# Retention and a cosine-gated MLP on one core: the second output weight is loaded earlier, block 3's retention is done in fewer visits, results get two buffers, loads run three blocks ahead

## The chip, the core and the metric

One core of one Trainium2 chip runs the whole program. The metric is the device time of one execution in microseconds (us), lower is better. Engines are named as in the profile: PE (TensorE's matmuls), PEld (its weight loads), DVE (VectorE), ACT (ScalarE), POOL (GpSimd) and SP (SyncE, which here only issues DMAs). Each engine works through its own instructions in the order in which the program lists them; engines wait for each other, and for DMAs, on semaphores.

## What is computed

Retention (attention with a decay in place of the softmax) for 8 batches, 8 heads, 576 positions and 64 features, and then a two-layer network on the 4608 tokens of 512 features. Types in and out are float32.

```python
def _attn_ref(q, k, v):
    scores = scale * np.matmul(q, k.transpose(0, 1, 3, 2))
    gamma = 1.0 - 2.0 ** (-5.0 - np.arange(H, dtype=np.float32))
    rel = pos[:, None] - pos[None, :]
    Dmat = np.where(rel >= 0, gamma[:, None, None] ** rel[None, :, :], 0.0)
    return np.matmul(scores * Dmat[None], v)

def _moe_ref(x, w_in, w_out):          # x: the retention's output, 4608 x 512
    h = x @ w_in                       # 512 -> 2048
    return (h * np.cos(h)) @ w_out     # 2048 -> 512
```

## The kernel before

**Tiling.** The tokens are cut in 18 blocks `j` of 256 (`BK`, two chunks of 128 each) for the retention, and in 9 stages `n` of 512 (`W`) for the network; stage n uses blocks 2n and 2n+1. Batches are 576 tokens long, so some chunks hold the end of one batch and the start of the next ("mixed", with masks and value tiles of their own: `mask_mix`, `mask_cmix`, `v_mix`, `v_odd`). Blocks 0 to 3 are laid out in pairs of positions (`c.pair`), later ones by chunk.

**A block's way.** `load` (L128) brings q, k and v into float32 tiles `fq`, `fk`, `fv` (pool `ld`, three buffers of each). `scaled` (L155) multiplies q and k by powers of the decay and rounds them to bf16 (`qks`); `prep` does that for all four parts on POOL. `transpose_dma` (L195) turns them by a DMA on SP, or `transpose_pe` (L203) on PE with an evacuation to `qkT` by ACT or DVE. `round_v` (L173) rounds v to `vb`. `scores` (L228) multiplies k by q into PSUM, and its two `masked` steps on DVE write `ret`. `sums_of` (L315) makes the state that is carried to the next chunk (`s32` on DVE, `sb` on ACT). `outputs` (L437) adds own and carried parts in PSUM and writes x (`xT`).

**The network.** `mm1` (L448) makes h for one part of a stage, ACT takes the sine (a shifted cosine), DVE multiplies (`gT`). For n = 0 the product with `w_out` is done directly (L878): 64 matmuls, with block 2's and block 3's retention steps placed in between by the list `todo`, which gives for each step the number of matmuls ahead of it. From n = 1 on, `mm2_seven` (L578) multiplies 2 x 2 quarters by seven products instead of eight, with sums of quarters of `gT` (`g_sum`, DVE, or POOL for sum 7 from n = 2 on) and of `w_out` (`w_sums`); results are gathered in tiles `ot` with tags a, b, c, d (pool `op`, one buffer of each tag) and stored by SP (`stored_rows`). The products run in the order 1, 2, 6, 4, 7, 5, 3; `at` says in front of which the retention steps of later blocks stand. `pend` holds DVE work and stores that `flush` issues later.

**What sets the order.** The schedule is written by hand (`manual_schedule`): program order is each engine's order. On SP the loads, the transposing DMAs and the stores stand in one queue. POOL issues the weights' DMAs (with the cast to bf16) between its own work. `step` (L645) does one block's preparation: `prep`, `transpose_dma`, `round_v` on POOL, and then `load_next`; `steps_to(j)` runs it up to block j - 1. At the start weights and loads are chained by `gate`s: block 2's load waits until the fourth part of `w_in` has landed (`w_dma[3]`), block 3's until the second part of `w_out` has (`w_dma[5]`). Four parts of `w_out` of four 128-row groups each are loaded (`load_w_out(0)`, `(4)`, `(8)`, `(12)`); the last two are issued after k and after q of block 2 are scaled (L779 to L782).

**Block 3** is turned on PE at the end of n = 0's products. Its scores are made in two visits, `scores_y` (L288), one for each parity of positions, inside the second and third part of n = 1's `mm1`, with two half-size DVE masks each; its sums stand in the fourth part, its outputs after that, and the fifth part is the first that needs its x.

```python
            if (n, i) == (1, 0):
                steps_to(5)
            ...
            steps_to({0: 7, 3: 8}.get(u, 0))                  # n = 1, after store u
            steps_to({0: 2 * n + 6, 2: 2 * n + 7}.get(u, 0))  # n > 1
```

The functions that the change touches, with the line numbers of the profile:

Of the kernel before, what the change touches and what calls it, by code (L numbers as in the profile page):

```python
# [17 lines left out]
def kernel(  # L18
# [10 lines left out]
    P = 128  # L29
# [34 lines left out]
    op = ctx.enter_context(tc.tile_pool(name="op", bufs=1))  # L64
# [9 lines left out]
    qpos_i = consts.tile([P, PERQ, 2, H], I32)  # L74
    qpos = consts.tile([P, PERQ, 2, H], F32)
    kpos_i = consts.tile([P, PERK, H], I32)
    kpos = consts.tile([P, PERK, H], F32)
    gq = consts.tile([P, PERQ, 2, H], F32)
    gkp = consts.tile([P, NP_B, 2, H], F32)
    gkc = consts.tile([P, PERK, H], F32)  # L80
    mask_p = consts.tile([P, 2, P], F32)
# [91 lines left out]
    def round_v(j, runs=(nc.gpsimd.tensor_copy,) * 2):  # L173
        f = tiles.pop(("fv", j))
        vb = nat.tile([P, 2, H, D], BF16, tag="vb", name="vb")
        for y in range(2):
            runs[y](vb[:, y], f[:, :, y, :] if j < NP_B else f[:, y])  # L177
        for c in chunks[j]:
            if c.mixed and c.pair:
                for y in range(2):  # L180
                    nc.gpsimd.tensor_copy(v_mix[HP // 2 : HP, y], f[HP // 2 : HP, :, y, :])
                    nc.gpsimd.tensor_copy(v_mix[HP:, y], f[HP:, :, y, :])
            elif c.mixed:
                nc.gpsimd.tensor_copy(v_odd[HP:], f[HP:, c.k])
        tiles["vb", j] = vb
# [101 lines left out]

    def scores_y(j, y, banks):  # L288

        cs = chunks[j]  # L290
        kT = tiles["qkT", j]
        if ("ret", j) not in tiles:
            tiles["ret", j] = retp.tile([P, 2, HG, 2, P], BF16, tag="ret", name="ret")
        ret = tiles["ret", j]
        mask = mask_mix if any(c.mixed for c in cs) else mask_p
        pss = [psum.tile([P, HG, P], F32, tag=t, name="sc") for t in banks]
        for hg in range(HG):
            for he in range(2):
                for c in cs:
                    nc.tensor.matmul(  # L300
                        pss[he][c.rows, hg, :],
                        lhsT=kT[he * D : he * D + D, 1, y, hg, c.rows],
                        rhs=q_cols(c, he, hg),
                        start=True,
                        stop=True,
                    )
        for he in range(2):
            nc.vector.tensor_tensor(
                out=ret[:, he, :, y, :],
                in0=pss[he],  # L310
                in1=mask[:, y].unsqueeze(1).to_broadcast([P, HG, P]),
                op=ALU.mult,
            )
# [461 lines left out]
    for r in range(2):  # L775
        late = slice(r * HP + HP // 2, r * HP + HP)
        nc.gpsimd.memset(mask_mix[: HP // 2, :, late], 0.0)
        nc.gpsimd.memset(mask_cmix[:HP, late], 0.0)
    for name in "kq":  # L779
        for y in range(2):  # L780
            scaled(nc.gpsimd, 2, name, y)
        w_dma += [load_w_out(8 + "kq".index(name) * 4)]  # L782
    round_v(2)
    load_next(names="kqv", gate=w_dma[5])
    load_next()
    prep(3)
    round_v(3)
# [20 lines left out]
    banks_of = {0: "mbmabmab", 1: "abmamabm"}  # L808
# [16 lines left out]

    def block3_sums():
        sums_of(3, "n")()()

    for n in range(NT):
        blocks = blocks_of.get(n) or [(e + k * E2, 0, W) for e in range(0, E2, 2) for k in range(2)]  # L830
        for i, (et, c0, cw) in enumerate(blocks):
            inside = {
                (0, 1): {1: block1_carried},
                (1, 1): {1: lambda: scores_y(3, 0, ("n", "st"))},
                (1, 2): {1: lambda: scores_y(3, 1, ("n", "st"))},
                (1, 3): {2: block3_sums},
# [6 lines left out]
            if (n, i) == (1, 3):  # L843
                outputs(3, "b")
                for e in range(0, E2, 2):
                    w_sums(7, e, e + 2)
            if (n, i) == (1, 4):
                steps_to(6)
            if (n, i) == (2, 2):
                steps_to(9)  # L850
            if n:
                sums_after(n, i)
        if n == 0:
# [5 lines left out]
                (12, lambda: transpose_pe(2, "k", "a", act)),  # L859
                (18, lambda: transpose_pe(2, "q", "b", act)),  # L860
                (24, block2_scores),
                (34, block2_sums),
                (46, lambda: outputs(2, "b")),
                (52, lambda: transpose_pe(3, "k", "a", act)),
                (59, lambda: transpose_pe(3, "q", "b", act)),
# [3 lines left out]
                for at, x, e in (  # L869
                    (4, 5, 0), (10, 5, 4), (50, 6, 0), (53, 6, 4), (57, 4, 0), (60, 4, 4)  # L870
# [3 lines left out]
            for done in range(4 * ET):  # L874
                while todo and todo[0][0] <= done:
                    todo.pop(0)[1]()
                e, t = divmod(done, 4)
# [7 lines left out]
            for t in range(4):  # L885
                ot = op.tile([P, 1, DM], F32, tag="abcd"[t], name="ot")
                (act, vec)[t % 2](ot[:, 0], pss[t])
                stored_rows(t * P, 0, DM, ot)
            load_next()
# [30 lines left out]
        def mid_unit(flush, pend):  # L920
            def then():
                flush()
                outputs(a, "m")

            intro(b, "ab", "st", pend, then)
# [16 lines left out]
        def stored(u):  # L942
            if n == 1:
                steps_to({0: 7, 3: 8}.get(u, 0))
            else:
                steps_to({0: 2 * n + 6, 2: 2 * n + 7}.get(u, 0))
# [32 lines left out]
```

## Time and profile before

The three timed runs took 313.01, 310.40 and 314.32 us: median 313.01. The profile is of one execution of its own.

| | |
|---|---|
| profiled execution, its time | 315.17 us |
| its span, first to last instruction | 313.5 us |
| mean granted TensorE clock | 0.976 of full |
| PE busy | 287.7 us (92%), 3256 instructions |
| DVE busy | 217.9 us (70%) |
| POOL busy | 151.7 us (48%) |
| ACT busy | 139.0 us (44%) |
| DMA moved | 49.78 MB, 159 GB/s over the span |
| q, k, v loads, stores, transposes (SP's queue) | 45.10 MB, 74.0% of the engines' time |
| weights (POOL's queue) | 4.19 MB, 8.2% |

Stages by PE, from the order of time (us from the span's start):

| stretch | what PE does |
|---|---|
| 0 to 17.6 | blocks 0 and 1 prepared, scored; weights arrive |
| 17.6 to 33.0 | first products of n = 0 |
| 33.0 to 56.5 | second products of n = 0, with blocks 2 and 3 between |
| 56.5 to 78.2 | first products of n = 1, with block 3's retention |
| 78.2 to 95.1 | second products of n = 1, with blocks 4 and 5 |
| 95.1 to 128.9 | n = 2 |
| 128.9 to 163.5 | n = 3 |
| 163.5 to 192.9 | n = 4; from here on each stage repeats this one |

How to read the lines further on. A row of the order of time has the start, the duration, the engine, the source line, the operation, what it writes and reads, the form, how many, and in brackets the idle time of the engine ahead of it with what ended it. A row of waits has who waited for whom, the total in us, how many times, and the longest. A row of windows has the stretch and its length, then busy us (and the instruction count) of PE, PEld, DVE, ACT and POOL, then the granted PE clock, the mean busy share of the 16 DMA engines (above 1 where packets overlap) and GB/s. When a wait was for several things, the row names the one that came last. A DMA row on SP (SPq) tells how long its issue took, not when the data landed.

### The profile page before, as it was taken

Reading aid. Unit: us, or ns where it says so; the run is one execution under the profiler, and the core shown is the slowest. Engines: PE = TensorE matmul, PEld = TensorE weight load, DVE = VectorE, ACT = ScalarE, POOL = GpSimd, SP = SyncE. Lnnn points to the kernel's source line nnn. Section 1 sums busy time; section 2 is a strip of 40 time slices with the busy share of each in tenths; the row PEclk is TensorE's granted clock in tenths of the full one; section 3 lists DMA queues with packets and bytes.
Section 4 is the critical chain, followed back from the end, with each engine's and each line's share of the span. In section 5 each row is a group of like instructions: output and inputs, shape, how many; then the busy total and the mean of one; then the engine's idle time right before and its main releaser. Section 6 shows DMA issues by size and latency. Waiting matters only on the chain.

```text
span 313.5 us, 7628 instructions
## 1 busy us (share of the span) xinstructions
PE 287.7 (92%) x3256; PEld 195.6 (62%) x3256; DVE 217.9 (70%) x267; ACT 139.0 (44%) x160; POOL 151.7 (48%) x180
## 2 busy tenths in 40 slices
PE   7689879879999988999599999999999999999991
PEld 3468534658875476547474587478648855874680
DVE  5656834565994997689365977797689669836931
ACT  4566413544344623365125633663364446326520
POOL 7830695942952974437902493269247113102300
PEclk9999998998999999999889999999999999999996
DMA  7999999699999999999998929995960630121014
GB/s 206 262 189 210 236 231 196 135 220 183 169 239 210 208 225 205 185 209 215 204 207 196 179 49 200 193 234 108 234 133 2 120 84 0 36 69 35 2 33 100
DMA packets 128930, 49.78 MB, mean 159 GB/s; under 512 B 89344, under 2 KB 128384, under 8 KB 128896
## 3 DMA queue, kind: packets, MB, share of 16 engines
q1 hardware_dynamic: 124672, 45.10, 74.0%
q0 software_dynamic: 4224, 4.19, 8.2%
q8 instruction: 25, 0.41, 0.6%
q14 instruction: 9, 0.07, 0.1%
HBM read 36.70 MB, written 9.44 MB: 147 GB/s over the span
## 4 chain that ended last, share of the span: by engine, by line
PE 66%; DMA 11%; DVE 10%; POOL 6%; issue 2%; ACT 2%; SPq 1%; DVEq 0%; POOLq 0%; ACTq 0%
PE h L458 29%; PE o L560 27%; DMA fk<-in_k_dram 5%; DVE gT L469 4%; POOL qks L166 4%; DMA w_in_sb<-in_moe_w_in_dram 3%; DMA w_out_sb<-in_moe_w_out_dram 3%; DVE gs L507 3%; PE o L878 3%; PE ov L388 2%; PE st L332 2%; ACT cosh L468 2%; DVE ret L278 2%; PE sc L268 1%; PE ov L420 1%
## 5 line engine op out<-in xcount | busy, mean ns | idle before, releaser
L458 PE MATMUL h<-xT,w_in_sb 128*128 128x512 bf16 (+1 forms) x704 | 128.8, 344 | 3.0 <-ACT xT L443 1.6
L469 DVE TENSOR_TENSOR gT<-h,cosh 128x1024 bf16<-128x1024 f32 x72 | 88.0, 1222 | 40.3 <-ACT cosh L468 40.1
L468 ACT ACTIVATE cosh<-h,half_pi 128x1024 f32<-128x1024 f32 x72 | 80.3, 1116 | 70.8 <-PE h L458 70.8
L458 PEld LDWEIGHTS <-w_in_sb 128*128 128x128 bf16 x704 | 69.2, 99 | 58.9 <-issue 1.5
L507 POOL TENSOR_TENSOR gs<-gT 128x512 bf16<-128x512 bf16 x28 | 35.8, 1282 | 96.4 <-DVE gT L469 96.4
L560 PEld LDWEIGHTS <-gs 128*128 128x128 bf16 x520 | 50.0, 99 | 11.3 <-issue 3.6
L166 POOL TENSOR_TENSOR qks<-fq,gq 128x512 bf16<-128x512 f32 x33 | 36.4, 1122 | 21.9 <-DMA fq<-in_q_dram 21.7
L560 PEld LDWEIGHTS <-gT 128*128 128x128 bf16 x384 | 37.1, 98 | 7.6 <-DVE gT L469 1.4
L590 ACT COPY ot<-o 128x512 f32<-128x512 f32 x32 | 18.7, 587 | 45.3 <-PE o L560 36.5
L560 PE MATMUL o<-w_out_sb,gs 128*128 128x256 bf16 (+1 forms) x264 | 32.2, 278 | 3.4 <-POOL qks L166 3.4
L586 DVE TENSOR_TENSOR ot<-ot,o 128x512 f32<-128x512 f32 x39 | 25.9, 681 | 12.4 <-ACT ot L590 7.9
L166 POOL TENSOR_TENSOR qks<-fk,gkc 128x512 bf16<-128x512 f32 x28 | 30.9, 1121 | 1.1 <-DMA fk<-in_k_dram 1.1
L560 PE MATMUL o<-w_out_sb,gT 128*128 128x256 bf16 x256 | 30.3, 273 | 1.1 <-DVE gT L469 1.1
L560 PE MATMUL o<-ws,gs 128*128 128x256 bf16 x256 | 30.8, 273 | 0.2 <-DVE gs L507 0.2
L278 DVE TENSOR_TENSOR ret<-sc,mask_c 128x1024 bf16<-128x1024 f32 x25 | 29.8, 1215 | 0.0
L177 POOL CAST vb<-fv 128x512 bf16<-128x512 f32 x33 | 21.5, 669 | 7.7 <-DMA fv<-in_v_dram 7.4
L443 ACT CAST xT<-ov 128x1024 bf16<-128x1024 f32 x16 | 16.2, 1012 | 15.6 <-PE ov L420 15.6
L362 DVE TENSOR_TENSOR s<-st,s 128x256 f32<-128x256 f32 x18 | 7.6, 423 | 17.2 <-PE st L332 16.8
L372 ACT CAST sb<-s 128x512 bf16<-128x512 f32 (+1 forms) x18 | 10.3, 575 | 18.7 <-DVE s L360 8.0
L878 PE MATMUL o<-w_out_sb,gT 128*128 128x512 bf16 x64 | 16.5, 401 | 2.2 <-DMA w_out_sb<-in_moe_w_out_dram 2.2
L507 DVE TENSOR_TENSOR gs<-gs,gT 128x1024 bf16<-128x1024 bf16 x16 | 15.8, 986 | 0.3
L560 PE MATMUL o<-ws,gT 128*128 128x256 bf16 x128 | 15.3, 272 | 0.0
(81 smaller groups left out, 199.3 us busy)
## 6 DMA issues: line engine op xcount, KB each, us to landing
out_dram<-ot SPq DMA_DIRECT2D x70, 128.0 KB, 2.6
fk<-in_k_dram SPq DMA_DIRECT2D x25, 256.0 KB, 5.5
fv<-in_v_dram SPq DMA_DIRECT2D x25, 256.0 KB, 5.9
fq<-in_q_dram SPq DMA_DIRECT2D x12, 512.0 KB, 4.9
w_in_sb<-in_moe_w_in_dram POOLq DMA_DIRECT2D x4, 512.0 KB, 8.3
w_out_sb<-in_moe_w_out_dram POOLq DMA_DIRECT2D x4, 512.0 KB, 11.2
fk<-in_k_dram SPq DMA_DIRECT2D x3, 512.0 KB, 7.1
fv<-in_v_dram SPq DMA_DIRECT2D x3, 512.0 KB, 7.3
```

Of the source, the lines that this page charges most:

```text
L166: return eng.tensor_tensor(out=dst.rearrange("p b a d -> p a b d"), in0=src.rearrange("p (a b) d -> p a b d", a=2), in1=by.rearrange("p (a ...
L177: runs[y](vb[:, y], f[:, :, y, :] if j < NP_B else f[:, y])
L278: nc.vector.tensor_tensor(out=ret[:, k].rearrange("p a b i -> p (a b) i"), in0=pss[k].rearrange("p a b i -> p (a b) i"), in1=mask.unsqueez ...
L443: evac(x, ps)
L458: nc.tensor.matmul(ps[:, j, :], lhsT=w_in_sb[:, dg, (et + j) * P : (et + j + 1) * P], rhs=xT[:, dg, c0 : c0 + w], start=(dg == 0), stop=(d ...
L468: nc.scalar.activation(cosh, ps, ACTF.Sin, bias=half_pi, scale=1.0)
L469: nc.vector.tensor_mul(gT[:, et : et + m, c0 : c0 + w], ps, cosh)
L507: eng.tensor_tensor(out=tiles["gs", n, x][:, e : e + step], in0=a[:, e : e + step], in1=b[:, e : e + step], op=op_,)
L560: nc.tensor.matmul(dst[i], lhsT=lhs[:, e, j * P : (j + 1) * P], rhs=rhs[:, e, c0:c1], start=(fresh and e == 0 and (i == 0 or len(parts) > 2)),
L586: return lambda: nc.vector.tensor_tensor(out=out_, in0=in0, in1=in1, op=ALU.add)
L590: nc.scalar.copy(t, tiles["all", x])
L878: nc.tensor.matmul(pss[t], lhsT=gT[:, e, t * P : (t + 1) * P], rhs=w_out_sb[:, e, :], start=(e == 0), stop=(e == ET - 1),)
```

## The change

- **Second weight ahead of the fourth block.** The third part of `w_out` is issued by POOL before block 2 is scaled, gated by the landing of the second part (`after`). The fourth part is issued between k and q of block 2. Block 3's load is gated by the third part (`w_dma[6]`) instead of the second. ("Fourth block" is block 3, counted from 1.)
- **Casts.** v of blocks 2 and 3 is rounded by ACT inside the list `todo`, not by POOL; `v_mix` is copied by DVE from the rounded tile in two copies, not by POOL from the float32 tile in four.
- **Retention of block 3 in fewer visits.** `scores_y` goes. All scores of block 3 are made at once after n = 0's products, with two full-size masks. Its sums move into the second part of n = 1's `mm1`, its outputs after the third part into bank `m`; the banks of that stage change.
- **n = 0's products.** The steps in `todo` move by some matmuls; the last quarter of the sum over rows of `w_out` is done result by result, and each of the four results is copied out when its last matmul is issued. The stores come after block 3's scores.
- **Two result buffers**: the pool `op` has two buffers of each tag. In exchange four small tiles used only at the start take the buffers of later `gs` tiles.
- **Loads three blocks ahead.** Blocks 5 and 6 are loaded from inside `todo`; before, block 5 was loaded after n = 0's stores. So each later `step` loads block j + 3 instead of j + 2.
- **Other places of preparations.** Block 8 is prepared after the last store of n = 1, not in the middle of n = 2's first products; block 7 after the third store; for n > 1 the second step of a stage comes after its last store instead of its third. `w_sums(7)` moves behind block 5's preparation.
- **Masks.** In n = 1 and 2 the second mask of the block scored in front of product 5 is no longer put off.

```diff
-    op = ctx.enter_context(tc.tile_pool(name="op", bufs=1))
+    op = ctx.enter_context(tc.tile_pool(name="op", bufs=2))
...
-    qpos_i = consts.tile([P, PERQ, 2, H], I32)
+    qpos_i = sump.tile([P, PERQ, 2, H], I32, tag="gs5", name="qpos_i")
...
             if c.mixed and c.pair:
-                for y in range(2):
-                    nc.gpsimd.tensor_copy(v_mix[HP // 2 : HP, y], f[HP // 2 : HP, :, y, :])
-                    nc.gpsimd.tensor_copy(v_mix[HP:, y], f[HP:, :, y, :])
+                nc.vector.tensor_copy(v_mix[HP // 2 : HP], vb[HP // 2 : HP])
+                nc.vector.tensor_copy(v_mix[HP:], vb[HP:])
...
+    w_dma.append(load_w_out(8))
+    after(w_dma[-1], w_dma[5])
     for name in "kq":
         for y in range(2):
             scaled(nc.gpsimd, 2, name, y)
-        w_dma += [load_w_out(8 + "kq".index(name) * 4)]
-    round_v(2)
-    load_next(names="kqv", gate=w_dma[5])
+        if name == "k":
+            w_dma.append(load_w_out(12))
+    load_next(names="kqv", gate=w_dma[6])
     load_next()
     prep(3)
-    round_v(3)
     prepared = 4
...
-    banks_of = {0: "mbmabmab", 1: "abmamabm"}
+    banks_of = {0: "mbmabmab", 1: "mababmab"}
...
+    def block3_scores():
+        for masked in scores(3, "ab"):
+            masked()
...
-                (1, 1): {1: lambda: scores_y(3, 0, ("n", "st"))},
-                (1, 2): {1: lambda: scores_y(3, 1, ("n", "st"))},
-                (1, 3): {2: block3_sums},
+                (1, 1): {1: block3_sums},
...
-            if (n, i) == (1, 3):
-                outputs(3, "b")
+            if (n, i) == (1, 2):
+                outputs(3, "m")
+            if (n, i) == (1, 4):
+                steps_to(6)
                 for e in range(0, E2, 2):
                     w_sums(7, e, e + 2)
-            if (n, i) == (1, 4):
-                steps_to(6)
-            if (n, i) == (2, 2):
-                steps_to(9)
...
-                (12, lambda: transpose_pe(2, "k", "a", act)),
-                (18, lambda: transpose_pe(2, "q", "b", act)),
-                (24, block2_scores),
-                (34, block2_sums),
+                (14, lambda: transpose_pe(2, "k", "a", act)),
+                (23, lambda: transpose_pe(2, "q", "b", act)),
+                (24, lambda: round_v(2, (act, act))),
+                (28, block2_scores),
+                (38, block2_sums),
                 (46, lambda: outputs(2, "b")),
+                (47, load_next),
+                (48, lambda: round_v(3, (act, act))),
                 (52, lambda: transpose_pe(3, "k", "a", act)),
-                (59, lambda: transpose_pe(3, "q", "b", act)),
+                (57, lambda: transpose_pe(3, "q", "b", act)),
+                (58, load_next),
...
-                    (4, 5, 0), (10, 5, 4), (50, 6, 0), (53, 6, 4), (57, 4, 0), (60, 4, 4)
+                    (4, 5, 0), (10, 5, 4), (44, 6, 0), (45, 4, 0), (50, 6, 4), (51, 4, 4)
...
-            for done in range(4 * ET):
+            part = 3 * ET // 4
+            order = [(t, e) for e in range(part) for t in range(4)]
+            order += [(t, e) for t in (2, 3, 0, 1) for e in range(part, ET)]
+            stores = []
+            for done, (t, e) in enumerate(order):
...
-            for t in range(4):
-                ot = op.tile([P, 1, DM], F32, tag="abcd"[t], name="ot")
-                (act, vec)[t % 2](ot[:, 0], pss[t])
-                stored_rows(t * P, 0, DM, ot)
-            load_next()
+                if e == ET - 1:
+                    ot = op.tile([P, 1, DM], F32, tag="abcd"[t], name="ot")
+                    (act, vec)[t % 2](ot[:, 0], pss[t])
+                    stores.append((t * P, ot))
+            block3_scores()
+            for r0, ot in stores:
+                stored_rows(r0, 0, DM, ot)
...
-            intro(b, "ab", "st", pend, then)
+            intro(b, "ab", "st", None, then)
...
-                steps_to({0: 7, 3: 8}.get(u, 0))
+                steps_to({0: 7, 2: 8, 3: 9}.get(u, 0))
             else:
-                steps_to({0: 2 * n + 6, 2: 2 * n + 7}.get(u, 0))
+                steps_to({0: 2 * n + 6, 3: 2 * n + 7}.get(u, 0))
```

## The prediction

> **What bounds the kernel now.** I read the chain of waits first, then who waits for whom, then the order of time between 33 and 164 us, and last the windows by stage. L(j) is the load of block j, T(j) its transposing DMA (L197), both on SP; times are us from the span's start.
>
> ```profile
> PE 66%; DMA 11%; DVE 10%; POOL 6%; issue 2%; ACT 2%; SPq 1%; DVEq 0%; POOLq 0%; ACTq 0%
> ```
>
> PE is the bound, but not everywhere. From 163.50 on one n of the main loop takes 29.44 (first-product starts 163.50, 192.94) and PE has no gap. Before that n=1 takes 38.6 (56.49 to 95.08), n=2 33.8, n=3 34.6. The change acts there, and the question is how much of each excess goes. The waits and the order of time name them:
>
> ```profile
> ACT ot L590 <- DMA out_dram<-ot: 7.0, 1, 7.0
> PE o L560 <- POOL qks L166: 3.4, 1, 3.4
> PE o L878 <- DMA w_out_sb<-in_moe_w_out_dram: 2.2, 1, 2.2
> PE h L458 <- ACT xT L443: 1.6, 1, 1.6
> ...
> 149.68 1.91 PE L560 MATMUL o<-ws,gT 128*128 128x256 bf16 x16
> 155.01 3.54 PE L560 MATMUL o<-w_out_sb,gs 128*128 128x256 bf16 x16 [3.42 <-POOL qks L166]
> ...
> 125.44 0.41 PE L388 MATMUL ov<-ret,vb 128*64 128x128 bf16 x8 [1.43 <-DVE ret L278]
> 111.47 1.70 PE L560 MATMUL o<-w_out_sb,gT 128*128 128x256 bf16 x14 [1.10 <-DVE gT L469]
> ```
>
> The first two rows are one event. In n=3 ACT's copy into `ot` (tag b) waits 7.0 until 154.38 for n=2's store of the same buffer, which SP issued behind T(10) and L(12) (issues from 140.69, the stores 149.96 to 153.17). PE can't add product 7 to the bank before that copy, so it stands 3.42; POOL is only who came last. The sixteen matmuls after it take 3.54, not 1.91: the clock falls after the gap.
>
> ```profile
> 70.00:74.00 4.00, 4.00 (x25) 2.99 (x24) 0.00 (x0) 0.79 (x1) 2.27 (x3) 0.62 1.08 160
> 156.00:160.00 4.00, 4.00 (x86) 2.80 (x83) 0.99 (x3) 0.92 (x2) 1.14 (x3) 0.70 1.00 201
> 124.00:126.00 2.00, 0.57 (x26) 0.47 (x27) 2.00 (x4) 0.00 (x0) 2.00 (x3) 1.00 1.33 218
> 126.00:130.00 4.00, 3.60 (x70) 2.47 (x59) 3.44 (x4) 1.32 (x2) 2.76 (x4) 1.00 1.00 181
> ```
>
> The clock (the column before the last two) is 0.62 after the 1.55 gap that ends at 69.58, 0.70 after the 3.42 one, and 1.00 after 1.43. So a PE gap of 1.55 or more costs 1.63 besides itself (3.54 - 1.91), one of 1.43 or less nothing. The Trainium skill, TensorE: Matmul & The Clock Gate, section on HAM oscillation, warns only of gaps above about 3.4 us; the 0.62 row speaks against it, and by the page the gaps I remove would be worth some 5 us less.
>
> The second limit is SP's one queue:
>
> ```profile
> 67.87 4.53 SPq L197 DMA_TRANSPOSE qkT<-qks  x1
> 72.46 0.62 POOL L177 CAST vb<-fv 128x512 bf16<-128x512 f32 x1 [0.32 <-DMA fv<-in_v_dram]
> 79.99 3.97 SPq L197 DMA_TRANSPOSE qkT<-qks  x1
> 84.47 1.02 POOL L177 CAST vb<-fv 128x512 bf16<-128x512 f32 x1 [0.18 <-DMA fv<-in_v_dram]
> 94.38 0.61 POOL L177 CAST vb<-fv 128x512 bf16<-128x512 f32 x1 [1.13 <-DMA fv<-in_v_dram]
> ...
> 55.50:58.50 3.00, 3.00 (x26) 2.21 (x24) 1.38 (x2) 1.99 (x3) 2.35 (x4) 1.00 0.13 27
> 64.00:72.40 8.40, 6.56 (x110) 4.77 (x108) 3.45 (x4) 3.64 (x4) 4.70 (x5) 0.84 1.16 203
> 84.40:94.40 10.00, 9.49 (x167) 7.94 (x166) 9.26 (x13) 4.55 (x7) 6.26 (x8) 1.00 1.19 227
> ```
>
> T(4)'s issue ends at 72.40, just when L(5)'s last v lands (the cast starts 72.46); T(5)'s at 83.96, as L(6) lands: a T waits for all that SP queued before it, then lands about 2 later. One L and one T take 10.4 (83.96 to 94.38), an L alone 7.6 (1.57 MB at 203 to 210 GB/s). Until 178 us the DMA engines are full, with one hole, 55.5 to 58.5 at 27 GB/s, in which SP waited for n=0's results to store.
>
> **Part by part.** (1) *Second weight.* L666 for rows 8 to 11 goes from POOL's place at 35.96 (landing 45.12) to just after rows 4 to 7 land (SP's gated L(3) shows that at 32.1). It then lands near 39 to 41 (first bytes 3.5 after its issue, then 0.52 MB at the 145 GB/s that its queue got between 40 and 46). POOL waits 13 us for that, beside a wait until 33.97 that it has anyway. PE's 2.17 at 45.16 goes, with the half clock behind it: 3.8. L(3) is now gated by this landing, so it starts near 40 instead of 32.14. That need not cost: L(2)'s v, and rows 12 to 15 issued at 36.0, fill the engines meanwhile, and the same 5.8 MB as before must pass from 29 to 55.5, so L(3) lands by about 49 to 51 and L(4) by 56 to 58 (before 57.9). By the queues' shares in 40 to 46 (POOL's 84.8% of the engines' time, SP's 34.2%) a weight goes ahead of a load, so block 2's v, which landed at 38.75, pays about 2.5. The Trainium skill, DMA: Bandwidth & Descriptors, section Queues, rings and completion order, has the engines take turns between the queues packet by packet; by that v would pay about half, and the weight would land a little later.
>
> (2) *Casts.* Four POOL casts (0.59 to 0.61) and four v_mix casts (0.61) leave POOL: 4.8 free, worth nothing by itself, for POOL then waits for L(3). Four ACT casts of 0.62 come, which wait for v; behind them in ACT stand the evacuations of block 3's transposes and the `ot` copies. With v(3) at 49 to 51, ACT has k and q out by 53 to 54.5. Two DVE copies of 1024 bf16 values: nearest rows 0.42 (512, from PSUM) and 0.69 (1024, two inputs); I take 0.4 each. They wait on DVE for ACT's cast of v(2) (near 42.5), and block 2's masks (2 x 1.2) stand behind them, done by 45.8; outputs(2) wants them at 46. Cover: 0.2; without it PE waits as long as v(2) is late, 1 to 2. The positions' tiles that now share `sump` buffers are read by 4 and overwritten at 65 at the earliest: nothing.
>
> (3) *n=0's products and block 3.* PE from 33.0: 64 matmuls at 0.214 to 0.23, 24 transposes and the rest of block 2 as before give 52.5; scores(3) waits for ACT until 53 to 54.5 and takes 0.64. First products of n=1 start at about 54 (before 56.49), and need 14.1 (128 at 0.11) + 0.75 sums + 1.4 outputs, for the two visits of scores (0.83 on PE, 1.0 of waits for DVE) are gone, and block 3's x is ready one whole product earlier, which removes the 1.55 and its 1.63. mm2 of n=1 could begin at 70.4, not 78.2: 7.8 on paper. DVE's four masks of 0.64 become two of 1.2: even.
>
> (4) *Loads three ahead.* This takes most of it back. Before T(4) SP now has L(5), L(6) and the eight stores; L(6) is new. From L(4) at 56 to 58: 7.6 + 7.6 + 2 to 4 for the stores puts T(4)'s issue at 74 to 77, landing 76 to 79 (before 74.2). The hole at 55.5 (3.0) is what this gains back. PE wants scores(4) at 74.3 (70.4 + 3.7 for two products + sums): a new wait of 2 to 4. T(5) comes 10.4 later, 86.4 to 89; PE would be there 9.3 after scores(4) (three products 5.75, sums and outputs 1.35, half clock 1.6, scores 0.6), so it waits again about 1. Scores(5) is at 86.4 to 88.5 against 89.25, and n=2 starts at 92.3 to 94.4 (5.8 later, as before) against 95.08: gain 0.7 to 2.8, taken 1.8. POOL's `w_sums(7)` (4 x 1.15) now stands behind block 5's preparation, ready about 71, wanted past 80: nothing, and it has 9 us of cover.
>
> (5) *n=2.* The second mask of blocks 5 and 7 is no longer put off behind the state sum that waits for PE: the 1.43 at 125.44 goes. Block 8's preparation leaves the middle of n=2, where POOL's own sums were late and DVE's took 1.08 and 1.62 beside them (0.69 at 173.01): the 1.10 at 111.47 goes, and 0.4 at 128.90 stays or goes. Gain 2.5. T(8) has to be there: T(5)'s issue 85.4 + 3 x 10.4 + 3 for stores = 119.6, landing 121.7; PE wants it at 93.3 + 28.4 = 121.7. No margin: 0 to 1 lost, 0.3 taken.
>
> (6) *Two result buffers.* n=3's copy meets a buffer last stored in n=1, and the step that stood before that store now follows it. 34.6 becomes 29.44, as in n=4, which has no such wait: gain 5.2. What is late next is nothing within that stage.
>
> Sum: 1.8 + 2.5 - 0.3 + 5.2 = 9.2. The profiled execution took 315.17 (span 313.5), 2.16 above the median 313.01, so 306.0 there and 303.8 on the median's footing; I say 304.
>
> **Rivals.** *A, the queue keeps the early gain.* If L's go at 182 GB/s (as in 72.4 to 84.4: 8.6 each), T(4)'s issue is at 58 + 17.2 + 4 = 79.2 and T(5) lands 11.4 + 2 later, 92.6: n=2 starts 3 late, and T(8) makes half of (5) void: 313.0 + 3 - 1.2 - 5.2 = 309.6, so 307 to 312. For: the 182 row. Against: 203 to 227 in the others.
>
> *B, slower: T(5) far behind.* L(3) behind the weight's landing, L(6) behind ACT's cast of v(3), T(4) behind both. It decides when scores(5) is past 89.25 + 7.4 + 6.3 = 103, 15 later than I have it. That takes L(3) starting 6 later (a weight held to 45 as before) and SP standing idle for one L more (7.6) while v(3) waits on ACT; then 319 to 324. Against: the engines were full in 40 to 46, so idle time must be new.
>
> *C, the early gain survives.* At 227 GB/s (6.9 an L) T(4)'s issue is at 56 + 13.8 + 2 = 71.8, T(5) lands 9.4 + 2 later, 83.2, and n=2 starts at 89, 6 early: 313.0 - 6 - 2.5 - 5.2 = 299.3, so 299 to 302.
>
> *D, the buffers move the wait*: ACT's copy then waits for something else in n=3; worth up to 5.2 back, 307 to 309. Against: n=4.
>
> **How the numbers follow.** Forecast 302 to 306.7: 0.50; C 0.11; A and D 0.23; B 0.16, 0.06 of it short of 2%. About 2% (6.3) is what a measurement of this kernel can tell from no change: faster (below 306.75) 0.61, within 0.29, slower 0.10. The range from C's 299.5 to near A's end, 311.5, leaves out some 0.2: most of B, the ends of A and C.
>
> **What would show it.** Right: no ACT wait on `out_dram<-ot`, n=3 at 29.5; T(4) landing after 74.2, PE waiting on scores(4) or (5) for a DMA; no gap at rows 8 to 11 of the weight. Wrong: first products of n=1 later than 56.5; scores(5) past 90; a new wait in n=2 on block 8; PE's clock below 1 in n=3.

## The result, and the profile after

The changed kernel took 310.2 us (median of 19 runs, 308.8 to 312.5), the kernel before 314.3 on the same chips: ratio 0.990, 95% interval 0.988 to 0.993. It is faster, by 1% where 2.9% was forecast. (Medians are of all runs; ratios and intervals leave out executions in a slower state, over 1.5% above the fastest of the same kernel.) The profiled execution took 312.25 (span 310.5, before 313.5).

Where the time went shows best in the starts of PE's stages, in the two profiled executions (us from the span's start; the forecast's lead is put together from its own terms):

| start of | before | after | lead forecast | lead measured |
|---|---|---|---|---|
| second products of n = 0 | 33.0 | 34.2 | 0 | -1.2 |
| first products of n = 1 | 56.5 | 55.9 | 2.5 | 0.6 |
| second products of n = 1 | 78.2 | 72.6 | 7.8 | 5.6 |
| n = 2 | 95.1 | 95.2 | 1.8 | -0.1 |
| n = 3 | 128.9 | 130.3 | 4.0 | -1.4 |
| n = 4 | 163.5 | 160.6 | 9.2 | 2.9 |
| end of the span | 313.5 | 310.5 | 9.2 | 2.9 |

The lead grows to 5.6, is lost altogether in 22 us, shrinks by another 1.3 in n = 2, and comes back by 4.3 in n = 3. From n = 4 on nothing changes. The chain's summary says what the end now waits for:

```profile
PE 68%; DMA 16%; POOL 5%; DVE 4%; issue 2%; ACT 2%; SPq 1%; DVEq 0%; POOLq 0%; ACTq 0%
```

DVE's share fell from 10% to 4%, and DMA's rose from 11% to 16%. Half of the 16% is the load of `w_out` (8%, before 3%), through which the chain now runs at the start; T's own share is 3%. What held PE is told by its waits (who for whom, total, times, longest):

```profile
PE sc L267 <- DMA qkT<-qks: 6.8, 3, 4.5
PE o L858 <- ACT ot L867: 2.2, 1, 2.2
...
PE h L430 <- DVE gT L441: 0.6, 1, 0.6
```

All three DMA waits are for a T. The rows of before that the prediction shows (the copy into `ot`, the weight, block 3's x) are gone from PE's waits, and one large row is new: a matmul of n = 0 waits 2.2 for a copy on ACT. The order of time, for PE, then ACT, then SP's queue:

```profile
52.16 1.24 PE L858 MATMUL o<-w_out_sb,gT 128*128 128x512 bf16 x5 [2.15 <-ACT ot L867]
...
81.00 1.07 PE L267 MATMUL sc<-qkT 64*64 64x128 bf16 x32 [4.54 <-DMA qkT<-qks]
...
89.80 0.64 PE L267 MATMUL sc<-qkT 64*64 64x128 bf16 x32 [0.21 <-DMA qkT<-qks]
...
125.95 1.07 PE L267 MATMUL sc<-qkT 64*64 64x128 bf16 x32 [2.03 <-DMA qkT<-qks]
...
50.49 1.14 ACT L177 CAST vb<-fv 128x512 bf16<-128x512 f32 x2 [1.27 <-DMA fv<-in_v_dram]
51.54 0.58 ACT L867 COPY ot<-o 128x512 f32<-128x512 f32 x1
...
65.24 4.53 SPq L149 DMA_DIRECT2D fv<-in_v_dram  x3
69.86 6.41 SPq L548 DMA_DIRECT2D out_dram<-ot  x8
76.37 2.30 SPq L196 DMA_TRANSPOSE qkT<-qks  x1
...
84.29 3.80 SPq L196 DMA_TRANSPOSE qkT<-qks  x1
...
120.15 3.67 SPq L196 DMA_TRANSPOSE qkT<-qks  x1
```

Read from the bottom. SP puts L(6) and then eight stores in front of T(4). L(6) lands at 72.48, the last store at 78.28, T(4)'s issue ends at 78.67 and it lands at 80.96; PE, ready at 76.46, waits 4.54 for it. T(5)'s issue ends at 88.09 and T(8)'s at 123.82, which lands at 125.91, 2.03 after PE wants it. The ACT rows explain the 2.15: the copy into `ot`, L867, stands in ACT's order behind the two casts of v(3), which wait for v(3) to land at 50.47. PE's next matmul writes the other half of the PSUM tile `two` that the copy reads from, and it does not start before the copy ends.

The windows (stretch, length, then busy us of PE, PEld, DVE, ACT and POOL; the granted clock is the column before the last two):

```profile
69.86:78.28 8.42, 6.60 (x67) 5.65 (x64) 8.28 (x10) 3.33 (x4) 6.54 (x7) 1.00 0.72 168
...
81.00:84.40 3.40, 3.40 (x44) 2.50 (x45) 2.71 (x3) 0.00 (x0) 0.80 (x1) 0.51 1.19 269
84.40:92.00 7.60, 7.39 (x125) 6.29 (x124) 4.34 (x6) 3.28 (x5) 5.33 (x6) 1.00 1.14 226
...
125.96:132.00 6.04, 5.82 (x51) 3.84 (x53) 3.04 (x3) 0.00 (x0) 0.00 (x0) 0.50 1.22 215
```

The stores' stretch moves 168 GB/s, less than the 203 and 227 of the loads' stretches that the prediction shows (its rival A names one of 182). After each wait the clock is at half, 3.41 us long the first time and 6.83 (125.29 to 132.12) the second, though that gap was the smaller.

### The profile page after: what moved, and what is told of

It is laid out like the page before. It is cut to its first block, busy times and chain, and to the rows that moved or that the text cites. A ratio compares the mean times of both kernels' runs of the same rounds, so it can differ in the third digit from the quotient of the medians.

```text
span 310.5 us, 7615 instructions
## 1 busy us (share of the span) xinstructions
PE 287.6 (93%) x3239; PEld 198.1 (64%) x3256; DVE 219.8 (71%) x267; ACT 140.7 (45%) x164; POOL 147.8 (48%) x172
## 3 DMA queue, kind: packets, MB, share of 16 engines
q1 hardware_dynamic: 124672, 45.10, 72.2%
## 4 chain that ended last, share of the span: by engine, by line
PE 68%; DMA 16%; POOL 5%; DVE 4%; issue 2%; ACT 2%; SPq 1%; DVEq 0%; POOLq 0%; ACTq 0%
PE h L430 32%; PE o L532 28%; DMA w_out_sb<-in_moe_w_out_dram 8%; POOL qks L166 4%; DMA qkT<-qks 3%; DMA fv<-in_v_dram 3%; DMA fk<-in_k_dram 2%; PE sc L267 2%; PE ov L360 2%; DVE gT L441 2%; PE st L304 1%; PE ov L392 1%; ACT cosh L440 1%; SPq L135 1%; PE o L858 1%
## 5 line engine op out<-in xcount | busy, mean ns | idle before, releaser
L430 PE MATMUL h<-xT,w_in_sb 128*128 128x512 bf16 (+1 forms) x690 | 127.5, 342 | 1.5 <-DVE gT L441 0.6
L441 DVE TENSOR_TENSOR gT<-h,cosh 128x1024 bf16<-128x1024 f32 x72 | 87.9, 1223 | 37.4 <-ACT cosh L440 37.2
L479 POOL TENSOR_TENSOR gs<-gT 128x512 bf16<-128x512 bf16 x28 | 35.7, 1277 | 105.5 <-DVE gT L441 103.6
L532 PEld LDWEIGHTS <-gs 128*128 128x128 bf16 x520 | 50.7, 100 | 8.0 <-issue 0.3
L166 POOL TENSOR_TENSOR qks<-fq,gq 128x512 bf16<-128x512 f32 x33 | 38.4, 1183 | 14.5 <-DMA fq<-in_q_dram 9.4
L532 PE MATMUL o<-ws,gs 128*128 128x256 bf16 x256 | 31.8, 279 | 0.0
L177 POOL CAST vb<-fv 128x512 bf16<-128x512 f32 x29 | 17.4, 624 | 1.6 <-DMA fv<-in_v_dram 1.6
L858 PE MATMUL o<-w_out_sb,gT 128*128 128x512 bf16 x61 | 14.6, 379 | 2.5 <-ACT ot L867 2.2
L267 PE MATMUL sc<-qkT 64*64 64x128 bf16 x448 | 9.6, 230 | 6.8 <-DMA qkT<-qks 6.8
L479 DVE TENSOR_TENSOR gs<-gT 128x512 bf16<-128x512 bf16 (+1 forms) x25 | 15.3, 612 | 0.4
```

The source lines that it names most:

```text
L166: return eng.tensor_tensor(out=dst.rearrange("p b a d -> p a b d"), in0=src.rearrange("p (a b) d -> p a b d", a=2), in1=by.rearrange("p (a ...
L430: nc.tensor.matmul(ps[:, j, :], lhsT=w_in_sb[:, dg, (et + j) * P : (et + j + 1) * P], rhs=xT[:, dg, c0 : c0 + w], start=(dg == 0), stop=(d ...
L441: nc.vector.tensor_mul(gT[:, et : et + m, c0 : c0 + w], ps, cosh)
L479: eng.tensor_tensor(out=tiles["gs", n, x][:, e : e + step], in0=a[:, e : e + step], in1=b[:, e : e + step], op=op_,)
L532: nc.tensor.matmul(dst[i], lhsT=lhs[:, e, j * P : (j + 1) * P], rhs=rhs[:, e, c0:c1], start=(fresh and e == 0 and (i == 0 or len(parts) > 2)),
L858: nc.tensor.matmul(pss[t], lhsT=gT[:, e, t * P : (t + 1) * P], rhs=w_out_sb[:, e, :], start=(e == 0), stop=(e == ET - 1),)
```

## The experiments

The theory: a T stands on SP behind everything queued before it, so the third load ahead delays T(4) and all later T by one L, and this gives back what the early edits gain; the two result buffers are most of what is left. Its rivals: the early edits gain nothing that lasts even without the third load; or what holds the kernel is the new wait on ACT, or the place of block 8, or the weight. All ratios are against the kernel before, run beside the kernel on the same chip (medians 314.0, 314.2 and 314.8 in the three groups of four runs). One table for all, with landings and starts from the profiles:

| kernel | T(4) | T(5) | T(8) | n=2 starts | n=4 starts | median us | ratio (95%) |
|---|---|---|---|---|---|---|---|
| before | 74.2 | 86.0 | 120.9 | 95.1 | 163.5 | 314.3 | 1 |
| after | 81.0 | 89.8 | 125.9 | 95.2 | 160.6 | 310.2 | 0.990 (0.988 to 0.993) |
| e1_two_ahead | 72.5 | 83.1 | 117.4 | 91.4 | 154.8 | 306.6 | 0.976 (0.972 to 0.981) |
| e2_before_two_buffers | 72.2 | 84.0 | 118.2 | 91.6 | 154.7 | 307.6 | 0.982 (0.975 to 0.988) |
| e3_after_one_buffer | 81.7 | 91.8 | 124.3 | 97.2 | 161.9 | 314.0 | 0.999 (0.995 to 1.003) |
| e4_transposes_on_act | 74.4 | 87.6 | 113.0 | 104.1 | 174.7 | 337.8 | 1.076 (1.070 to 1.081) |
| e5_two_ahead_v3_on_pool | 72.0 | 84.9 | 117.6 | 90.2 | 153.6 | 303.7 | 0.971 (0.964 to 0.978) |
| e6_block8_behind_sums | 71.7 | 82.9 | 118.3 | 88.3 | 150.6 | 302.2 | 0.965 (0.959 to 0.971) |
| e7_after_v3_on_pool | 79.7 | 88.5 | 124.7 | 94.6 | 158.1 | 309.6 | 0.989 (0.985 to 0.992) |
| e8_two_buffers_masks | 71.6 | 83.4 | 118.0 | 91.1 | 156.3 | 307.4 | 0.982 (0.976 to 0.988) |
| e9_weight_old_place | 70.3 | 81.0 | 117.3 | 88.1 | 149.6 | 302.3 | 0.963 (0.957 to 0.969) |
| e10_t5_ahead_of_load6 | 72.4 | 76.4 | 119.2 | 87.9 | 152.6 | 303.4 | 0.964 (0.959 to 0.969) |
| e11_masks_put_off | 72.0 | 84.6 | 116.8 | 91.4 | 153.3 | 305.3 | 0.966 (0.960 to 0.973) |
| e12_before_three_ahead | no record | 91.8 | no record | 99.5 | 161.5 | 312.1 | 0.992 (0.988 to 0.996) |

### The third load ahead: e1 and e12

The changed kernel without its second extra load:

```diff
                 (57, lambda: transpose_pe(3, "q", "b", act)),
-                (58, load_next),
```

> The changed kernel without the load of block 6 inside n = 0's products, so that every later step loads j + 2 as before the change. Theory Q (the gain is eaten because T(4) and T(8) stand behind one more load in SP's queue): T(4) lands near 70 to 72 instead of 80.96, PE has no DMA wait at scores(4) or scores(8), n = 2 starts near 90 instead of 95.4, and the time is 6 to 10 us below the changed kernel's 310.2 (300 to 304). Rival R (the DMA engines' throughput is the limit, so the order in the queue only moves the wait): T(4) is earlier, but T(5) and T(8) are not earlier than 88 and 124, PE waits there instead, and the time stays within 1.5 us of 310.2.

It is faster than the changed kernel: 0.976 against 0.990, intervals apart, some 4.4 us, less than the 6 to 10 expected. In its order of time:

```profile
52.47 1.24 PE L857 MATMUL o<-w_out_sb,gT 128*128 128x512 bf16 x5 [2.42 <-ACT ot L866]
...
108.73 2.36 PE L532 MATMUL o<-w_out_sb,gT 128*128 128x256 bf16 x20 [2.00 <-DVE gT L441]
...
67.90 2.18 SPq L196 DMA_TRANSPOSE qkT<-qks  x1
...
77.56 3.58 SPq L196 DMA_TRANSPOSE qkT<-qks  x1
```

T(4)'s issue ends at 70.08 and not 78.67, 8.6 earlier, one L; no scores wait for a DMA any more. n = 2 starts 3.8 earlier although the wait on ACT (2.42) is still there, with a half clock behind it this time. So T(4) is late in the changed kernel because of the extra load. What is next: the wait on ACT, and 2.00 on DVE in n = 2.

The other direction needs a kernel without the other edits: the kernel before with two buffers (e2, below), plus one load:

```diff
             load_next()
+            load_next()
             continue
```

> e2 (the kernel before with two result buffers, 307.6) with one more load, block 6, ahead of T(4) in SP's queue, nothing else of the change. Theory Q: T(4) lands near 80 instead of 72.2 and T(8) near 126 instead of 118.2; PE wants scores(4) at 78.5 and scores(8) at 122.4, so it waits about 1.5 to 4 at each, with half clocks: 4 to 8 us above e2, 311 to 315. Rival: the extra load costs only where PE comes early as in the changed kernel; here PE is late enough, and the time is within 1.5 of e2.

The ratio is 0.992 against e2's 0.982 (intervals just touching), 312.1 against 307.6 us in the medians. The order of time has the same picture as the changed kernel:

```profile
81.49 0.64 PE L268 MATMUL sc<-qkT 64*64 64x128 bf16 x32 [1.94 <-DMA qkT<-qks]
91.80 1.07 PE L268 MATMUL sc<-qkT 64*64 64x128 bf16 x32 [3.27 <-DMA qkT<-qks]
```

Both scores wait for their T, T(5) lands at 91.8 against 84.0 in e2, and n = 2 starts at 99.5 against 91.6. T(4)'s landing is not recorded in e12, but its issue ends at 79.45 against 70.56 in e2, and T(5) lands 7.8 later. So the delay by one load does not come from the other edits.

### The result buffers: e2 and e3

e2 is the kernel before with only this (and the four small start tiles in the buffers of `gs`, as in the change):

```diff
-    op = ctx.enter_context(tc.tile_pool(name="op", bufs=1))
+    op = ctx.enter_context(tc.tile_pool(name="op", bufs=2))
```

> The kernel before with two result buffers alone (and the four start tiles in the later tiles' buffers). By the prediction's term for the buffers n = 3 takes 29.4 instead of 34.6, and the time is 5.2 us below the kernel before, a ratio near 0.983. If the wait only moves (rival D), ACT or PE shows a new wait in n = 3 and the gain is under 2.5 us.

Ratio 0.982, some 5.8 us (1.2% to 2.5%); n = 3 takes 29.4 instead of 34.6. (Its profiled execution is 8.8 ahead at n = 4. The 3.6 beyond n = 3's share come earlier, where the half clocks that the kernel before had after its gaps at 45 and 70 did not come; they are not put down to the buffers.) These few words alone do as much as the whole change or more (0.982 against 0.990, intervals touching). The reverse, the changed kernel with one buffer of each tag:

```diff
-    op = ctx.enter_context(tc.tile_pool(name="op", bufs=2))
+    op = ctx.enter_context(tc.tile_pool(name="op", bufs=1))
```

> The changed kernel with one result buffer again. If the second buffer alone removed n = 3's stall, it comes back in n = 3 (about 5 us, 315). If the moved step (the store now stands ahead of the next block's transposing DMA and load) does it too, n = 3 stays at 29.5 to 30; but n = 1's last store now lands at 124.05 behind the load of block 10, after n = 2's copy into the same buffer at 117.2, so a wait appears in n = 2 instead, partly beside PE's wait for T(8): 2 to 5 us above 310.2.

Ratio 0.999, no difference from the kernel before; against 0.990 the second buffer is worth some 2.7 us in the changed kernel, half of what e2 has. The wait is back, but one stage earlier:

```profile
122.59 1.91 PE L532 MATMUL o<-w_out_sb,gs 128*128 128x256 bf16 x16 [3.36 <-POOL qks L166]
```

That is in n = 2 (before: the same gap at 155.01, in n = 3), and again ACT's copy behind it waits 3.94 on `out_dram<-ot`. Which stage meets the store depends on where the queue stands; with one buffer one stage does. Behind this wait PE comes to scores(8) later and does not wait for T(8) any more, so that n = 2 takes 35.3 in this profile and 35.1 in that of the changed kernel: one wait stands in the place of the other. Where the 2.7 lies is not shown.

### T on another queue: e4

The theory says that T waits only because SP's queue stands in front of it. The changed kernel with T issued by ACT:

```diff
         new_qkT(j)
-        nc.sync.dma_start(
+        nc.scalar.dma_start(
```

> The changed kernel with the transposing DMAs issued by ACT instead of SP, all else alike. Theory Q: T(4) no longer waits for loads 5 and 6 and the stores; it lands within 3 to 6 us of ACT's place for it (before 70), T(8) before 110, no PE wait for a DMA at scores(4) and scores(8), and the time is 300 to 305. Rival R: the engines are full, T lands late on any queue, and the time is within 1.5 us of 310.2. Against both: each issue stops ACT for as long as the transposing DMA waits for the engines; then ACT's sines come late and the time is above 310.

T(4) does land earlier, 74.4 against 81.0, but the kernel takes 1.076 of the time before. ACT's part of the order of time:

```profile
69.06 1.40 ACTq L196 DMA_TRANSPOSE qkT<-qks  x1
70.51 0.62 ACT L344 CAST sb<-s 128x512 bf16<-128x512 f32 x1 [8.35 <-POOL w_out_sb L459]
...
79.37 3.54 ACTq L196 DMA_TRANSPOSE qkT<-qks  x1
83.33 2.12 ACT L440 ACTIVATE cosh<-h,half_pi 128x1024 f32<-128x1024 f32 x2 [2.91 <-DVE gs L479]
...
86.36 4.18 ACTq L196 DMA_TRANSPOSE qkT<-qks  x1
...
97.91 5.07 ACTq L196 DMA_TRANSPOSE qkT<-qks  x1
...
103.30 4.06 ACTq L196 DMA_TRANSPOSE qkT<-qks  x1
107.46 1.11 ACT L440 ACTIVATE cosh<-h,half_pi 128x1024 f32<-128x1024 f32 x1 [3.42 <-issue]
```

Issuing a T holds ACT's own queue 1.4 to 5.1 us, and the sines and copies behind it are late. The issue is not all of it: around T(4) ACT computed nothing for 8.35, of which the issue is 1.40, and the row puts the wait down to POOL, which makes T's input; PE then waits 4.95, until 71.19, for the `sb` behind it. How the loss divides between the two was not tried. On SP the same issue holds up only other DMAs, so of the two queues SP is the better place for T; what stands ahead of it there is the question.

### The wait on ACT: e5 and e7

v(3) rounded on POOL behind `prep(3)`, as before the change, once in e1 and once in the changed kernel:

```diff
     prep(3)
+    round_v(3)
     prepared = 4
...
                 (47, load_next),
-                (48, lambda: round_v(3, (act, act))),
```

> Loads two blocks ahead as in e1, and v of block 3 rounded by POOL behind the preparation of block 3, not by ACT inside n = 0's products. In e1 PE stands 2.42 at 50.04 because the next matmul into the tile that holds two of the four results waits for ACT's copy of the first, and ACT waits for v(3). Theory: that gap goes, with the half clock that e1 shows behind it; n = 1 starts at 54 to 55.5 instead of 57.8, and the time is 2 to 4 us below e1's 306.6. Rival: T(4) (landing 72.5 in e1) then bounds scores(4), and less than 1 us is left.

> The changed kernel, loads three ahead, with v of block 3 rounded by POOL. It takes away the 2.15 wait at 50.01 alone. Theory Q: n = 1 starts 2 earlier, but scores(4) stays at T(4)'s landing, 80 to 81.5, so the wait there grows by as much and the time stays within 1.2 us of the changed kernel's 310.2. Rival: the unforeseen wait on ACT is what the forecast missed, and 2 to 4 us come back.

In both the gap at 50 is gone, and first products of n = 1 start at 54.3 and 54.6, where the prediction had them ("about 54"). With two loads ahead the median falls by 2.9 (306.6 to 303.7; the ratios' intervals, 0.971 and 0.976, overlap). With three ahead it falls by 0.6 (0.990 to 0.989), no difference that these runs can tell. There PE reaches scores(4) 1.3 earlier, T(4) also lands 1.3 earlier, and the wait is 4.59, with a half clock of 6.83 behind it; n = 2 starts 0.6 earlier. The wait on ACT is real, and with three ahead the wait for T(4) takes its place. With two ahead T(4) holds nothing up, but PE, now earlier, waits for T(5), which it had not done in e1:

```profile
84.91 0.64 PE L267 MATMUL sc<-qkT 64*64 64x128 bf16 x32 [3.00 <-DMA qkT<-qks]
```

### The place of block 8, and the masks: e6, e8, e11

e5 has a gap of 1.34 in n = 2 that comes from DVE's sums (L479), which take 1.39 and 1.63 beside POOL's work. e6 moves block 8's preparation behind them:

```diff
             if n:
                 sums_after(n, i)
+            if (n, i) == (2, 6):
+                steps_to(9)
...
-                steps_to({0: 7, 2: 8, 3: 9}.get(u, 0))
+                steps_to({0: 7, 2: 8}.get(u, 0))
```

> As e5, and block 8's preparation placed behind POOL's own sums in n = 2, not after the last store of n = 1. In e1 DVE's two sums beside POOL's take 1.63 and 1.62 instead of 0.68, and PE waits 2.00 for DVE at 106.7. Theory: POOL does its sums before DVE's, DVE's take about 0.7, the 2.00 goes and T(8), which stands behind load 9 anyway, lands no later than 119 (wanted at 120 or later): 1 to 2.5 us below e5. Rival: the two engines' sums overlap all the same, or T(8) comes late: within 0.7 of e5.

In n = 2 of e5, and then of e6, the order of time has these DVE rows:

```profile
101.60 1.39 DVE L479 TENSOR_TENSOR gs<-gs,gT 128x1024 bf16<-128x1024 bf16 x1
...
104.05 1.63 DVE L479 TENSOR_TENSOR gs<-gT,gs 128x1024 bf16<-128x1024 bf16 x1
```

```profile
99.56 0.68 DVE L479 TENSOR_TENSOR gs<-gs,gT 128x1024 bf16<-128x1024 bf16 x1
101.29 0.68 DVE L479 TENSOR_TENSOR gs<-gT,gs 128x1024 bf16<-128x1024 bf16 x1
```

The same instruction on the same tiles costs 0.68 or 1.63. In e5 POOL runs `scaled` from 97.95 to 102.4 and its own sums from 103.98 for 5.12, so it is at work when DVE's sums start. In e6 its sum there starts at 99.72, 0.16 after DVE's first, and it is POOL's that takes longer, 1.53 against 1.15 for its sum at 96.14; beside DVE's second POOL is idle, from 101.25 to 103.19. The Trainium skill, SBUF — State Buffer, section "SBUF: two separate sides", has DVE with two SBUF inputs and a GpSimd operation that reads SBUF lock a port pair against each other, and the one that starts later waits; the rows agree. The gap on the sums is gone, and the best version so far results: 302.2 us, 0.965. Against e5 (0.971) the intervals overlap; against the changed kernel and e1 they do not. What is left in PE's way is T again:

```profile
82.97 0.64 PE L267 MATMUL sc<-qkT 64*64 64x128 bf16 x32 [1.00 <-DMA qkT<-qks]
118.34 0.64 PE L267 MATMUL sc<-qkT 64*64 64x128 bf16 x32 [1.30 <-DMA qkT<-qks]
```

Then the masks that are no longer put off, alone on e2 (e8), and undone in e6 (e11):

```diff
-            intro(b, "ab", "st", pend, then)
+            intro(b, "ab", "st", None, then)
```

> The kernel before with two result buffers (e2, 307.6) and the second mask of the block scored ahead of product 5 no longer put off. The prediction's term: the 1.43 gap at the outputs of block 7 (120.38 in e2) goes and nothing else moves: 1.0 to 1.8 us below e2. Rival: DVE only shifts the wait, so that another stands behind it: within 0.5 of e2.

> e6 with the second mask of the block scored ahead of product 5 put off again, as in the kernel before. The prediction's term: a gap of 1.43 in front of block 7's outputs near 116, 1.0 to 1.8 above e6. Rival (as e8 on e2 suggested): PE then arrives later at scores(8), whose T(8) it waits for anyway (1.30), so the two overlap and the time is within 0.5 of e6.

In e8 the 1.43 shrinks to 0.32 and the time stays, 307.4 against 307.6: another wait of 2.17 comes at 106.47, for DVE's sums took 1.45, 1.63 and 1.62 there against 0.69, 0.95 and 1.08 in e2. In e11 the 1.43 comes back, and the ratio is 0.966 against e6's 0.965: no difference that these runs can tell. (The median of all its runs is higher, 305.3, and its profile has T(5) 1.7 later, which the masks don't explain.) That the masks are worth anything was not shown.

### The weight: e9

e6 with both parts of the weight issued where they were, and block 3 gated as before:

```diff
-    w_dma.append(load_w_out(8))
-    after(w_dma[-1], w_dma[5])
     for name in "kq":
...
-        if name == "k":
-            w_dma.append(load_w_out(12))
-    load_next(names="kqv", gate=w_dma[6])
+        w_dma += [load_w_out(8 + "kq".index(name) * 4)]
+    load_next(names="kqv", gate=w_dma[5])
```

> e6 (302.2) with the third and fourth part of the output weight issued where the kernel before does it, and block 3's load gated by the second part again. The prediction's part (1): PE waits about 2 for the weight's rows 8 to 11 near 43, with or without a half clock behind it, 2 to 3.8 us above e6. Rival: block 3's load starts 8 earlier (32 instead of 41), its v and block 4's come earlier, and the whole chain of loads and transposing DMAs moves up by 1 to 3, so scores(5) loses its wait and the time is within 1 of e6 or below.

0.963 against e6's 0.965: no difference. Rows 8 to 11 land at 43.84, later than the 41.52 of the changed kernel, and PE waits for them only briefly:

```profile
43.88 1.46 PE L856 MATMUL o<-w_out_sb,gT 128*128 128x512 bf16 x6 [0.29 <-DMA w_out_sb<-in_moe_w_out_dram]
```

In the kernel before, PE was ready for them at 42.99 and they landed at 45.12; here it is ready at 43.59 and they land 1.3 earlier. Why they do was not tried. In exchange L(3) is issued at 31.2 (41.6 in the changed kernel), T(5) lands at 81.0 against e6's 82.9, and scores(5) loses its wait, as the rival said. On balance the change's first item buys nothing here.

### T(5) ahead of L(6): e10

If the early T are late by the loads in front, the order can be changed instead of the depth. In e6, no load after the step of block 4, two after that of block 5:

```diff
             prepared += 1
-            load_next()
+            if prepared == 6:
+                load_next()
+            if prepared != 5:
+                load_next()
```

> e6 with T(5) ahead of load 6 in SP's queue (load 6 and 7 follow T(5)). Theory Q: T(5) lands near 74 to 76 instead of 82.9, PE's 1.00 wait at scores(5) goes, block 6's preparation on POOL comes no later than 90, T(6) about where it was; 0.5 to 1.5 us below e6. Rival: load 6 is then late, and T(8) (118.3 in e6, waited for 1.30) moves by 1 to 3: 0 to 2 above e6.

T(5) lands at 76.4 and scores(5) no longer waits, but the time is e6's: 0.964. T(6) lands at 95.0 as in e6, T(8) at 119.2 against 118.3, and PE waits there 2.65, with a half clock behind, where it had waited 1.30. Moving T(5) forward did not bring T(8) forward: the same bytes still stand ahead of it.

## Why the prediction was wrong in size

Its sign was right, the measured time lies inside its range, and its account of what the queue does was right; the sum was 9.2 where 2.9 came. By the table of starts, the 6.3 that are missing arose so: 1.9 ahead of n = 2, 3.5 in n = 2 and 0.9 in n = 3. The steps that failed are (4), which priced the stores in front of T(4) too low, and (5), which priced a missed T(8) at 0.3. Of the prediction's four signs of being wrong two came: a wait in n = 2 on block 8 (2.03), and a half clock at the start of n = 3. Point by point:

**(1) Weight.** "It then lands near 39 to 41": 41.52. L(3) landed at 50.5 ("49 to 51") and L(4) at 57.4 ("56 to 58"). The 2.17 did go, as forecast, but in e9, with the weight at its old place, 0.29 of it is left and the time is the same. Block 2's v was to pay "about 2.5" for the weight. It landed at 39.69 against 38.75, 0.9 later. The view of 40 to 46 us from which the queues' shares were read has 856 packets of the weight and 926 of the loads, so the shares of time do not show that a weight goes ahead of a load.

**(2) Casts.** Here the step named the right instructions and asked the wrong question: it put "the `ot` copies" behind the casts of v(3), and followed k and q out "by 53 to 54.5", but priced no PE wait on a copy. PE waited 2.15. In the medians that is 0.6 with the third load (e7) and 2.9 without it (e5), neither clear of the noise by itself.

**(3) n = 0's products and block 3.** The length of n = 1's first products was forecast as 14.1 + 0.75 + 1.4, that is 16.3, and took 16.7 (before 21.7). (The step counts 24 transposes in n = 0; the rows have 32, which at 0.45 for 8 is 0.45 more.) They started at 55.9 instead of 54; 1.3 of that is the wait above (e7: 54.6). The -1.2 that the stage had on entry is a half clock from 12.65 to 19.48; 8 of the 13 other profiles have one of that length there too, e2's among them, whose start is that of the kernel before but for four buffers, so it is not put down to the change.

**(4) Loads three ahead, the first failed step.** The mechanism was right ("This takes most of it back"), its size was not: "2 to 4 for the stores" was 5.8, from L(6)'s landing at 72.48 to the last store's at 78.28. The profile before had the price already: SP issues the same eight stores there from 57.15 on, and the last of them lands at 64.04, 6.2 after L(4).

```profile
57.15 5.03 SPq L576 DMA_DIRECT2D out_dram<-ot  x8
```

It put T(4)'s landing at "76 to 79"; it was 80.96. The new wait "of 2 to 4" was 4.54, scores(5) came at 89.8 and not "86.4 to 88.5", and the lead at n = 2 was -0.1 in place of 1.8. The step also counted the filled hole (3.0) as what the third load buys. e1 says that it buys nothing: there the first load from `todo` alone fills the hole (281 GB/s from 55.5 to 58.5, before 27).

**(5) n = 2, the largest error.** The gaps of 1.10, 1.43 and 0.40 went as forecast, save 0.32 of the 1.43. But T(8) was to land at 121.7, just when PE wants it: "No margin: 0 to 1 lost, 0.3 taken." T(8) landed at 125.9, 4.2 late: 2.7 were T(5)'s (issue end 88.09 against 85.4), and the three cycles to T(8), forecast as 3 x 10.4 + 3, took 12.0, 11.4 and 12.35, together 1.5 more. PE waited 2.03. The half clock then ran for 6.83: 4.4 us of it in n = 2 behind the gap, which at half speed costs about 2.2, and 1.8 in n = 3, about 0.9. So n = 2 took 35.1 and not 31.6 (33.8 - 2.5 + 0.3). A step with no margin should have been given the price of missing it, gap and clock, and not 0.3.

**(6) Two result buffers.** Forecast 5.2; e2 measured some 5.8 with it alone, e3 against the changed kernel some 2.7. In the change n = 3 took 30.3, the 0.9 above 29.4 being the clock left over from n = 2.

**The price of a gap**, taken from four gaps ("1.55 or more costs 1.63 besides itself, one of 1.43 or less nothing"), does not hold. Over eleven profiles (before, after, e1, e2, e3, e5, e7, e8, e10, e11, e12; e6 and e9 have no gap so long, and e4, with T on ACT, is left out) PE had 24 gaps of 1.41 to 3.42 after its first products began; the clock fell in or just behind 10 of them. It fell with 1.41 (e7) and 1.55 (before), and not with 1.55 in e2, 3.00 in e5 or 3.36 in e3. Gaps of 3.70, 4.54 and 4.59 all had it. It lasted 3.41 or 6.83.

**The rivals.** A ("the queue keeps the early gain", 307 to 312) is what happened, in effect and in time, though not by its own price: L(5) and L(6) took 15.1 together, as the forecast had it (2 x 7.6) and not A's 17.2; the stores took longer, and T(8) was missed. B did not come: scores(5) was at 89.8, not past 103. C, the early gain surviving (299 to 302), did not come; nearest to it is e6, the change with two loads ahead and two of its other edits placed differently, at 302.2. D falls with e2.

So the account by runs: the buffers bring some 5.8 to the kernel before (e2), and 2.7 are left of that in the change (e3). The third load takes some 4.4 of what the change would have (e1). What the rest of the change does shows in e1 against e2, 0.976 to 0.982, intervals overlapping: two waits, v(3) on ACT and DVE's sums beside POOL, kept its early gain from showing. With both mended (e6) it stands clear of e2: 302.2 against 307.6. How much of that belongs to block 3's fewer visits alone was not tried.

## What to carry to other kernels

Before you prefetch one block deeper, list what stands on the same queue behind the new load and when its consumer wants it: here one more load made the transposing DMAs 6 to 9 us later (the changed kernel against e1, e12 against e2), and a second queue for them cost more than it freed. A term with "no margin" is a bet at two prices, so write down the price of losing it (the wait, then the clock). And try the parts of a bundle alone: one of these parts did as much as the bundle or more.

## What the runs showed of the hardware

- Whether a gap of 1.4 to 3.4 us halves PE's clock is not settled by its length: 10 of 24 did. The Trainium skill, TensorE: Matmul & The Clock Gate, Part 1, describes a window of 3.413 us that runs free of the kernel. The lengths here, 3.41 and 6.83, are one and two of it, and a free-running window would make the same gap cheap in one run and dear in another, as 1.55 was. Its rule in HAM oscillation, that gaps above about 3.4 matter, names only those that always did here (3 of 3 above 3.42); of the shorter ones, which it leaves out, 10 of 24 cost too.
- On SP the issue of a transposing DMA ended about when the last DMA queued before it landed: in the changed kernel 78.67 against 78.28 for T(4), 88.09 against 88.03 for T(5), 100.08 against 99.74 for T(6), 123.82 against 124.05 for T(8). On ACT (e4), where no load or store stood in the queue, the issue still took 1.4 to 5.1 us; what it waited for there is not shown.
- Eight stores of 128 KB (1.05 MB) added 5.8 us to the queue, 181 GB/s; the loads ahead of them, 1.57 MB each, took 6.8 (L(5), 232 GB/s) and 8.3 (L(6), 190 GB/s).
